# Attention, MoE and MLP in one kernel: query tiles of two chunks in reverse order, their causal mask added by GpSimd

## The chip, the cores and the metric

One NeuronCore of a Trainium2 chip runs the whole program. The metric is device time in microseconds, the median of several executions. The engines are TensorE (PE; its weight loads are listed as PEld), VectorE (DVE), ScalarE (ACT), GpSimd (POOL) and SyncE (SP, which here only issues DMAs).

## The reference, cut to what matters

```python
scores = (1/sqrt(D)) * q @ k^T                 # B, H, S, D = 2, 8, 576, 64
cum    = cumsum(log(clip(f, 1e-4, 1)), -1)
scores = scores + cum[:, :, :, None] - cum[:, :, None, :]
scores = where(j > i, -1e9, scores)            # causal mask
attn   = softmax(scores);  x = attn @ v        # x: 1152 tokens x 512
x      = sum_e p_e * relu(x @ w1[e]) @ w2[e]   # 4 experts, F = 1024
out    = gelu_sigmoid(x @ w_in) @ w_out        # d_ff = 2048
```

The term with the query's own `cum` is constant along a row, so softmax drops it: only the key side is added.

## The kernel before

Attention is cut into four chunks of queries: chunks 0 and 2 are rows 0 to 255 of batch 0 and 1, chunks 1 and 3 rows 256 to 575. Chunk 0 goes first, head by head, by a path of its own ("plain", `first_step`). The rest goes by pairs of heads: four pairs of chunk 1, then four pairs that hold chunks 2 and 3 of batch 1. A pair of chunk 1 or 3 has three units, one for each tile of 128 queries: q0 = 256 (384 keys), 384 (512 keys) and 512. The last holds 64 queries of each head side by side and all 576 keys, in two pieces of 288.

A unit passes through these steps, named here as in the rows: scores `s` (PE, line 652, products with a high and a low part of q, `qhi` and `qlo`); the maximum (DVE, line 682), which adds the gate rows to the scores, writes `e` and returns `mx`; exp (ACT, line 698); the norm (POOL, line 708, multiplies `e` by `sm`, the inverse sum); transposes `t` (PE, line 726); copies `ph` (ACT); the product with v, `x` (PE, line 756). The gate rows are `cum` broadcast over the partitions by DMA: `cb` (512 keys, one for each head, for the tiles below 512) and `cbs` (576 keys, two halves of 64 partitions, for the tile q0 = 512). `load_cum` loads them two units ahead of a pair; `cb` has four buffers, `cbs` two, so a pair's rows reuse those of the pair two before.

The mask before is a matmul: line 655 adds `identr` x `tri` (128x128, -1e10 above the diagonal) onto the diagonal block of the scores, `tri2` in the tile q0 = 512, and line 657 does both heads at once where there are at most 256 keys (chunk 2).

POOL also makes the pairs' operands: `ks` (line 578, low part of the keys, half on DVE), `qhi` (line 68) and `qlo` (line 596), three units ahead. Scores of a tile with over 256 keys take both of the two PSUM buffers `ps_s`.

Expert products fill PE between the units: first layer `m<-xh,whi` and its like (lines 951, 934), second layer line 1099. Their weights are split into `whi` (ACT, line 71) and `wlo` (DVE, line 249; four in chunk 0 on POOL). A scheduler sets the order on each engine when the program is built; an engine then runs its instructions strictly in that order.

Of the kernel before, what the change touches and what calls it, by code (L numbers as in the profile page):

```python
# [7 lines left out]
F32 = mybir.dt.float32  # L8
# [7 lines left out]
B, H, S, D = 2, 8, 576, 64  # L16
# [4 lines left out]
CH = [(0, 0, SA), (0, SA, SB), (1, 0, SA), (1, SA, SB)]  # L21
# [8 lines left out]
REST = EXP[2]  # L30
QW = {1: 768, 2: 512, 3: 768}
LEAD = 3
NTILE = NT // 128
NBLK = 12
NMOE = 8
# [15 lines left out]
def attn_moe_mlp(ctx: ExitStack, tc: tile.TileContext, qk0, qk1, qk2, v0, vp, fg, dp, wa_moe, wb_moe, wa_mlp, wb_mlp, out):  # L51
# [6 lines left out]
    nc = tc.nc  # L58
# [5 lines left out]
    def f(ap):  # L64
        return ap.bitcast(F32)
# [9 lines left out]
    def load(out, in_):  # L75

        ins = nc.sync.dma_start(out=out, in_=in_)
        if start[0]:
            tc.keep_in_program_order(ins)
# [44 lines left out]
    cb_p = pool("cb", 4, scope=att_scope)  # L124
    cbs_p = pool("cbs", 2, scope=att_scope)
# [3 lines left out]
    cumd = pool("cumd", 1, bass.MemoryType.DRAM).tile([16, S], F32, name="cumd")  # L129
# [12 lines left out]
    tri = ac.tile([128, 128], F32R, name="tri")  # L142
# [24 lines left out]
    seq = [(1,) + units[0], (2,) + units[0], (1,) + units[1]]  # L167
# [4 lines left out]
    for v_ in range(v_exp, len(visits)):  # L172
        b, cs = visits[v_]
# [327 lines left out]
    pass_of = {c: p for p in passes for c in p[0]}  # L501
    groups, heads, pairs = {}, {}, {}

    def plain(c):


        return c == 0
# [90 lines left out]
    def load_cum(p, h0):  # L598

        cs, b, s0 = p  # L600
        st = pairs[p, h0]
        r = b * H + h0
        st["cb"] = [cb_p.tile([128, 512], F32, tag="cb", name="cb") for _ in range(2)]
        for g, cb in enumerate(st["cb"]):
            load(cb, cumd[r + g:r + g + 1, :512].to_broadcast([128, 512]))
        st["cbs"] = cbs_p.tile([128, S], F32, tag="cbs", name="cbs")
        for g in range(2):
            load(st["cbs"][64 * g:64 * g + 64], cumd[r + g:r + g + 1, :].to_broadcast([64, S]))

    def units_of(c, h0):  # L610

        if plain(c):
            return [(c, ((h,), (0, 128))) for h in (h0, h0 + 1)]
        _, s0, n = CH[c]
        return [(c, ((h0, h0 + 1), (q0,))) for q0 in range(s0, s0 + n, 128)]

    sc, raw_s = {}, {}
    NEG = -1.0 / D ** 0.5
# [1 line left out]
    def emit_scores(c, u):  # L620


        hs, tiles = u
        out = []
        for q0 in tiles:
            w = min(q0 + 128, S)
            if plain(c):
                st = heads[c, hs[0]]
                mm = [(0, w, [(st["qd"][:, q0:q0 + 128], st["kd"][:, :w])])]
            else:  # L630
                p = pass_of[c]
                st = pairs[p, hs[0]]
                (hi, lo), o = st["qs", c], 2 * (q0 - CH[c][1])
                zs = [(0, w, (0,)), (0, w, (1,))] if q0 < 512 else [(0, 288, (0, 1)), (288, S, (0, 1))]
                mm = [(a, z, [(t[:, o + 128 * g:o + 128 * g + 128], st["ks"][:, g, a:z]) for g in gs for t in (hi, lo)])
                      for a, z, gs in zs]
            pts = []
            both = not plain(c) and w <= 256
            for a, z, _ in mm:
                if plain(c):  # L640
                    if q0 == 0:
                        bank = ps_s.tile([128, 512], F32, tag="s", name="s")
                    pts.append(bank[:, q0:q0 + w])
                else:
                    if not both or not pts:
                        bank = ps_s.tile([128, 512], F32, tag="s", name="s")
                    pts.append(bank[:, 256:256 + w] if both and pts else bank)
                out.append((q0, w, a, z, pts[-1]))
            n = len(mm[0][2])
            for i in range(n):  # L650
                for pt, (a, z, lr) in zip(pts, mm):
                    nc.tensor.matmul(pt[:, :z - a], lhsT=lr[i][0], rhs=lr[i][1], start=i == 0 and not (both and pt is not bank),  # L652
                                     stop=i == n - 1, skip_group_check=both)
                    if i == 0 and z == w and not plain(c) and not both:
                        nc.tensor.matmul(pt[:, q0 - a:w - a], lhsT=identr, rhs=tri2 if w == S else tri, start=False, stop=False)
                if both and i == 0:
                    nc.tensor.matmul(bank.rearrange("p (g k) -> p g k", g=2)[:, :, q0:w], lhsT=identr,
                                     rhs=tri.unsqueeze(1).to_broadcast([128, 2, 128]), start=False, stop=False,
                                     skip_group_check=True)
        raw_s[c, u] = out  # L660
# [193 lines left out]
    def attention():  # L854


        seq = unit_seq
        first, last = {}, {}
        for i, (c, u) in enumerate(seq):
            for h in u[0]:  # L860
                first.setdefault((pass_of[c], h - h % 2), i)
                last[c, h] = i
        first_q = {}
        for i, (c, u) in enumerate(seq):
            if True:
                first_q.setdefault((pass_of[c], u[0][0], c), i)
        nxt = list(first)
        per_unit = dict(scores=emit_scores, max=emit_max, exp=emit_exp, norm=emit_norm, tr=emit_tr)
        by_last = dict(pv=emit_pv, x2=emit_x2)
        names = sorted(STAGES, key=lambda k: -STAGES[k])  # L870
        for i in range(len(seq) + L_X2 + 1):
            done = None
            new = [k for k in nxt if first[k] == i + LEAD]
            new_q = [k for k, j in first_q.items() if j == i + LEAD]
            last_pool = [j for j in nc.cur_bb.bb.instructions if j.engine == nc.gpsimd.engine][-1]
            with tc.issue_after(last_pool) if i == 0 else ExitStack():
                for k in new:
                    prep_parts(*k)
                for k in new_q:
                    prep_queries(*k)  # L880
            for k in [k for k in nxt if first[k] == i + 2]:
                load_cum(*k)
            for k in [k for k in nxt if first[k] == i and i]:
                load_values(*k)
            for k in names:
                j = i - STAGES[k]
                if k in per_unit:
                    if 0 <= j < len(seq):
                        per_unit[k](*seq[j])
                    continue  # L890
                fn, at = by_last[k], last
                for key in list(at):
                    if at[key] == j:
                        fn(*key)
                        if k == "x2" and key[1] == H - 1:
                            done = key[0]
            for k in new:
                n = nxt.index(k) + 1
                if n < len(nxt):
                    load_heads(*nxt[n])  # L900
            yield done
# [615 lines left out]
```

## Time and profile before

| | |
|---|---|
| median of 3 runs (range) | 691.7 us (691.58 to 691.74) |
| profiled execution | 691.82 us |
| its span | 690.1 us |
| instructions | 11086 |
| PE busy | 681.2 us |
| POOL busy | 239.4 us |
| DVE busy | 531.4 us |

The span is what the profile of one execution covers; 1.7 us lie outside it. Matmuls are pipelined and their ends are modelled, so a busy PE isn't PE at its peak: progress is read from the starts of its instructions.

### The profile page before, as it was taken

How to read it: one execution, taken by the hardware profiler on the slowest of the kernel's cores; microseconds unless marked ns; L12 is line 12 of the kernel's file. 1: busy time of each engine (PE TensorE's matmuls, PEld its weight loads, DVE VectorE, ACT ScalarE, POOL GpSimd, SP SyncE). 2: the span in 40 equal slices, each digit the busy share in tenths (PEclk: the TensorE clock that was granted, in tenths of full speed). 3: DMA queues.
4: the chain of work that ended last, by engine and by line, in shares of the span. 5: the costliest groups of instructions: out<-in, count | busy, mean ns of one | idle time of the engine just before them, and what ended most of it. 6: DMA issues, size and time to landing. Idle time of an engine off the chain costs nothing.

```text
span 690.1 us, 11086 instructions
## 1 busy us (share of the span) xinstructions
PE 681.2 (99%) x3937; PEld 600.0 (87%) x3937; DVE 531.4 (77%) x1097; ACT 354.3 (51%) x821; POOL 239.4 (35%) x286
## 2 busy tenths in 40 slices
PE   8999999999999999999999999999999999999997
PEld 4797888888888998998889898898899998998986
DVE  6896777777789688676887878767799989998632
ACT  5778767667543645635246254362456454452420
POOL 6887576532233454543035324133003300120000
PEclk9999999999999999999999999999999999999999
DMA  8697726313542244144631422403332544441012
GB/s 251 229 301 249 258 93 238 99 61 93 168 138 61 51 134 129 48 128 157 196 107 47 144 86 82 146 33 107 123 107 77 153 138 136 154 153 61 1 47 91
DMA packets 41063, 87.59 MB, mean 127 GB/s; under 512 B 3720, under 2 KB 5776, under 8 KB 40752
## 3 DMA queue, kind: packets, MB, share of 16 engines
q1 hardware_dynamic: 40680, 84.75, 38.2%
q0 software_dynamic: 288, 2.10, 0.8%
q8 instruction: 31, 0.51, 0.3%
q14 instruction: 24, 0.20, 0.1%
q10 hardware_dynamic: 40, 0.04, 0.0%
HBM read 73.98 MB, written 12.88 MB: 126 GB/s over the span
## 4 chain that ended last, share of the span: by engine, by line
PE 92%; DVE 4%; POOL 1%; ACT 1%; DMA 1%; issue 1%; SPq 0%; POOLq 0%; DVEq 0%
PE m L1099 41%; PE m L974 23%; PE m L934 15%; PE s L652 4%; PE x L756 4%; PE t L726 3%; PE m L1255 1%; DMA dpraw<-in_dp_dram 1%; DVE acc L1143 0%; POOL ks L578 0%; DVE hl L1088 0%; DVE cvd L431 0%; DVE wlo L249 0%; PE m L951 0%; DVE wf L433 0%
## 5 line engine op out<-in xcount | busy, mean ns | idle before, releaser
L1099 PE MATMUL m<-whi,hh 128*128 128x512 f32 x392 | 109.6, 392 | 0.0
L1099 PE MATMUL m<-wlo,hh 128*128 128x512 f32 x392 | 108.0, 391 | 0.0
L1099 PE MATMUL m<-whi,hl 128*128 128x512 f32 x392 | 107.2, 390 | 0.0
L249 DVE TENSOR_TENSOR wlo<-wst,whi 128x512 fp32r<-128x512 f32 x132 | 100.3, 774 | 5.1 <-ACT whi L71 4.6
L985 POOL TENSOR_TENSOR hl<-jc,hh 128x320 fp32r<-128x320 f32 (+1 forms) x60 | 53.1, 888 | 141.1 <-ACT hh L71 141.1
L71 ACT ACTIVATE whi<-wst 128x512 fp32r<-128x512 f32 x136 | 80.7, 625 | 23.7 <-PE m L1099 13.5
L1099 PEld LDWEIGHTS m<-wlo,hh 128*128 128x128 f32 x392 | 73.4, 188 | 15.5
L1099 PEld LDWEIGHTS m<-whi,hl 128*128 128x128 f32 x392 | 73.5, 188 | 15.5
L1099 PEld LDWEIGHTS m<-whi,hh 128*128 128x128 f32 x392 | 71.9, 188 | 12.4
L270 POOL TENSOR_TENSOR sr<-wst 128x256 f32<-128x256 f32 x20 | 17.9, 893 | 156.2 <-DMA wst<-wm 58.0
L708 POOL TENSOR_SCALAR e<-e,sm 128x128 f32<-128x128 f32 (+4 forms) x72 | 46.7, 660 | 60.3 <-DVE sm L706 35.9
L983 ACT ACTIVATE jc<-jc 128x320 f32<-128x320 f32 (+1 forms) x60 | 27.1, 451 | 54.8 <-DVE jc L980 54.3
L1143 DVE SCALAR_TENSOR_TENSOR acc<-m,dpn,acc 128x512 f32<-128x512 f32 x63 | 46.5, 744 | 9.0 <-PE m L1099 8.9
L934 PE MATMUL m<-xh,whi 128*128 128x256 f32 (+2 forms) x256 | 51.7, 316 | 0.0
L934 PE MATMUL m<-xl,whi 128*128 128x256 f32 (+2 forms) x256 | 51.7, 316 | 0.0
L934 PE MATMUL m<-xh,wlo 128*128 128x256 f32 (+2 forms) x256 | 51.0, 313 | 0.0
L698 ACT ACTIVATE e<-e,mx 128x128 f32<-128x128 f32 (+4 forms) x72 | 41.7, 581 | 11.6 <-DVE mx L682 11.1
L934 PEld LDWEIGHTS m<-xh,whi 128*128 128x128 f32 x256 | 41.6, 189 | 1.4
L934 PEld LDWEIGHTS m<-xl,whi 128*128 128x128 f32 x256 | 41.5, 189 | 0.8
L1082 ACT ACTIVATE m<-m 128x384 f32<-128x384 f32 x48 | 23.0, 480 | 37.3 <-DVE m L980 35.6
L934 PEld LDWEIGHTS m<-xh,wlo 128*128 128x128 f32 x256 | 41.5, 189 | 0.7
L71 ACT ACTIVATE ph<-t 128x256 f32<-128x256 f32 (+4 forms) x81 | 28.9, 405 | 17.6 <-PE t L726 17.2
(173 smaller groups left out, 1502.5 us busy)
## 6 DMA issues: line engine op xcount, KB each, us to landing
wst<-in_wa_moe_dram SPq DMA_DIRECT2D x28, 512.0 KB, 3.8
wst<-in_wb_moe_dram SPq DMA_DIRECT2D x28, 512.0 KB, 4.5
mst<-in_wa_mlp_dram SPq DMA_DIRECT2D x16, 512.0 KB, 3.7
wm<-wf SPq DMA_DIRECT2D x32, 256.0 KB, 3.9
mst<-in_wb_mlp_dram SPq DMA_DIRECT2D x16, 512.0 KB, 4.1
wst<-wm SPq DMA_DIRECT2D x16, 512.0 KB, 3.9
cb<-cumd SPq DMA_DIRECT2D x16, 256.0 KB, 4.0
qr<-in_qk_dram SPq DMA_DIRECT2D x8, 384.0 KB, 5.1
```

Of the source, the lines that this page charges most:

```text
L71: return nc.scalar.activation(out=out, in_=in_, func=AF.Copy)
L249: (nc.gpsimd if v_ == 0 and kind == 'a' and g < 4 else nc.vector).tensor_sub(lf, raw, f(hf))
L652: nc.tensor.matmul(pt[:, :z - a], lhsT=lr[i][0], rhs=lr[i][1], start=i == 0 and not (both and pt is not bank), stop=i == n - 1, skip_group ...
L698: nc.scalar.activation(out=e[:, off:off + w], in_=e[:, off:off + w], func=AF.Exp, scale=-1.0, bias=mx, accum_out=sm[:, 0, k:k + 1])
L708: nc.gpsimd.tensor_scalar(out=e[:, off:off + w], in0=e[:, off:off + w], scalar1=sm[:, 0, i:i + 1], scalar2=1.0, op0=ALU.mult, op1=ALU.mult)
L756: nc.tensor.matmul(pt[64 * g:64 * g + 64, o:n], lhsT=lhsT, rhs=rhs, start=i == 0, stop=i == nk - 1)
L934: nc.tensor.matmul(p[:, :n], lhsT=w[:, k, :], rhs=x[c][:, k, :], start=(j == 0 and k == 0), stop=(j == 2 and k == 3))
L974: nc.tensor.matmul(p[:, :WN], lhsT=w[a][:, k, :], rhs=x[z][:, k, :], start=start and j == 0 and k == 0, stop=stop and j == 2 and k == 1, s ...
L983: nc.scalar.activation(out=r, in_=r, func=AF.Relu)
L985: nc.gpsimd.tensor_sub(hl[:, g, :], r, f(hh[:, g, :]))
L1099: nc.tensor.matmul(p, lhsT=h_tile(v_, b, c, j, x, k), rhs=wb[v_, k][w].rearrange("p a c -> p (a c)"), start=i == 0 and k == 0, stop=i == 2 ...
L1143: nc.vector.scalar_tensor_tensor(out=a, in0=p, scalar=d, in1=a, op0=ALU.mult, op1=ALU.add)
```

## The change

The tiles of chunks 1 and 3 (`MASKED`) run from last to first: 512, 384, 256. For the tiles 384 and 256 the mask matmul goes. Instead POOL adds `tri` in place to the diagonal block of both `cb` (`mask_next`), one tile ahead: when the unit q0 = 512 is begun, to columns 384 to 511; when the unit 384 is begun, to columns 256 to 383. A later (lower) tile doesn't read the columns that were masked for the one before it, since it has 128 keys fewer. The add for 256 has to wait until DVE's maximum of the tile 384 has read those columns without the mask, and the maximum of 256 waits for the add. The tile 512 keeps its matmul with `tri2`. In chunk 1 `cbs` is now loaded ahead of `cb`; in the pairs of batch 1, which begin with chunk 2, `cb` stays first.

```diff
--- before.py
+++ after.py
@@ -30,6 +30,7 @@
 REST = EXP[2]
 QW = {1: 768, 2: 512, 3: 768}
 LEAD = 3
+MASKED = (1, 3)
 NTILE = NT // 128
 NBLK = 12
 NMOE = 8
@@ -600,19 +601,32 @@
         cs, b, s0 = p
         st = pairs[p, h0]
         r = b * H + h0
-        st["cb"] = [cb_p.tile([128, 512], F32, tag="cb", name="cb") for _ in range(2)]
-        for g, cb in enumerate(st["cb"]):
-            load(cb, cumd[r + g:r + g + 1, :512].to_broadcast([128, 512]))
-        st["cbs"] = cbs_p.tile([128, S], F32, tag="cbs", name="cbs")
-        for g in range(2):
-            load(st["cbs"][64 * g:64 * g + 64], cumd[r + g:r + g + 1, :].to_broadcast([64, S]))
+        def load_long():
+            st["cb"] = [cb_p.tile([128, 512], F32, tag="cb", name="cb") for _ in range(2)]
+            for g, cb in enumerate(st["cb"]):
+                load(cb, cumd[r + g:r + g + 1, :512].to_broadcast([128, 512]))
+
+        def load_last():
+            st["cbs"] = cbs_p.tile([128, S], F32, tag="cbs", name="cbs")
+            for g in range(2):
+                load(st["cbs"][64 * g:64 * g + 64], cumd[r + g:r + g + 1, :].to_broadcast([64, S]))
+
+        for fn in (load_long, load_last) if cs[0] == 2 else (load_last, load_long):
+            fn()
 
     def units_of(c, h0):
 
         if plain(c):
             return [(c, ((h,), (0, 128))) for h in (h0, h0 + 1)]
         _, s0, n = CH[c]
-        return [(c, ((h0, h0 + 1), (q0,))) for q0 in range(s0, s0 + n, 128)]
+        return [(c, ((h0, h0 + 1), (q0,))) for q0 in range(s0, s0 + n, 128)[::-1 if c in MASKED else 1]]
+
+    def mask_next(c, u):
+
+        q0 = u[1][0] - 128
+        if c in MASKED and q0 >= CH[c][1]:
+            for cb in pairs[pass_of[c], u[0][0]]["cb"]:
+                nc.gpsimd.tensor_add(cb[:, q0:q0 + 128], cb[:, q0:q0 + 128], f(tri))
 
     sc, raw_s = {}, {}
     NEG = -1.0 / D ** 0.5
@@ -651,7 +665,7 @@
                 for pt, (a, z, lr) in zip(pts, mm):
                     nc.tensor.matmul(pt[:, :z - a], lhsT=lr[i][0], rhs=lr[i][1], start=i == 0 and not (both and pt is not bank),
                                      stop=i == n - 1, skip_group_check=both)
-                    if i == 0 and z == w and not plain(c) and not both:
+                    if i == 0 and z == w and not plain(c) and not both and (c not in MASKED or w == S):
                         nc.tensor.matmul(pt[:, q0 - a:w - a], lhsT=identr, rhs=tri2 if w == S else tri, start=False, stop=False)
                 if both and i == 0:
                     nc.tensor.matmul(bank.rearrange("p (g k) -> p g k", g=2)[:, :, q0:w], lhsT=identr,
@@ -894,6 +908,8 @@
                         fn(*key)
                         if k == "x2" and key[1] == H - 1:
                             done = key[0]
+            if i < len(seq):
+                mask_next(*seq[i])
             for k in new:
                 n = nxt.index(k) + 1
                 if n < len(nxt):
```

The counts of built instructions differ in two forms alone: 32 matmuls `s<-tri,identr` 128x128 are gone from PE, and 32 adds `cb<-cb,tri` 128x128 are new on POOL. The order changes on every engine. Three places:

POOL at the end of chunk 0, where it normalizes the last heads (`e<-e,sm`) and makes the last `wlo`. Before:

```order
L249 TENSOR_TENSOR wlo<-wst,whi 128x512
L708 TENSOR_SCALAR e<-e,sm 128x128
L708 TENSOR_SCALAR e<-e,sm 128x256
L249 TENSOR_TENSOR wlo<-wst,whi 128x512
L708 TENSOR_SCALAR e<-e,sm 128x128
```

Now:

```order
L250 TENSOR_TENSOR wlo<-wst,whi 128x512
L629 TENSOR_TENSOR cb<-cb,tri 128x128
L722 TENSOR_SCALAR e<-e,sm 128x128
L722 TENSOR_SCALAR e<-e,sm 128x256
L250 TENSOR_TENSOR wlo<-wst,whi 128x512
L629 TENSOR_TENSOR cb<-cb,tri 128x128
L690 MEMSET e 128x64
L722 TENSOR_SCALAR e<-e,sm 128x128
```

Two adds (pair 1's first ones, each behind the landing of its `cb`) and a memset now stand ahead of norms of chunk 0.

POOL in the pairs of chunk 1, from pair 2's `qlo` (the second `qlo` buffer) on. Before:

```order
L596 TENSOR_TENSOR qlo_1_133<-qr,qhi 64x3x128 x2
L708 TENSOR_SCALAR e<-e,sm 128x384 x2
L708 TENSOR_SCALAR e<-e,sm 128x512 x2
L68 TENSOR_SCALAR qhi<-qr 128x768
L578 TENSOR_TENSOR ks<-kq,ks 64x576
L596 TENSOR_TENSOR qlo_0_132<-qr,qhi 64x3x128 x2
L708 TENSOR_SCALAR e<-e,sm 128x576
```

Now:

```order
L597 TENSOR_TENSOR qlo_1_133<-qr,qhi 64x3x128 x2
L629 TENSOR_TENSOR cb<-cb,tri 128x128 x3
L722 TENSOR_SCALAR e<-e,sm 128x576
L629 TENSOR_TENSOR cb<-cb,tri 128x128
L690 MEMSET e 128x64
L69 TENSOR_SCALAR qhi<-qr 128x768
L629 TENSOR_TENSOR cb<-cb,tri 128x128
L597 TENSOR_TENSOR qlo_0_132<-qr,qhi 64x3x128 x2
L579 TENSOR_TENSOR ks<-kq,ks 64x576
L722 TENSOR_SCALAR e<-e,sm 128x512 x2
```

Of the first three adds two are pair 2's for its tile 384; the third and the fourth are pair 1's for its tile 256. The add behind `qhi` is pair 3's: it waits for a `cb` of pair 3, and pair 3's `qlo` and `ks` and pair 1's norms (128x512, its tile 384) are behind it.

PE at pair 1's second and third unit. Before:

```order
L652 MATMUL s<-ks,qhi 128x512
L655 MATMUL s<-tri,identr 128x128
L652 MATMUL s<-ks,qlo_0_132 128x512
L1099 MATMUL m<-whi,hh 128x512 x2
L652 MATMUL s<-ks,qhi 128x288
```

Now:

```order
L666 MATMUL s<-ks,qhi 128x512
L666 MATMUL s<-ks,qlo_0_132 128x512
L666 MATMUL s<-ks,qhi 128x384
L666 MATMUL s<-ks,qlo_0_132 128x384
L1115 MATMUL m<-whi,hl 128x512 x4
L950 MATMUL m<-xh,whi 128x256 x4
L950 MATMUL m<-xh,wlo 128x256 x4
L950 MATMUL m<-xl,whi 128x256 x4
L740 MATMUL t<-identr,e 128x128 x5
```

The mask's 128-column matmul no longer stands between the high and the low product, and the five transposes of the tile 512 are now the first of the pair.

## Rows read from the trace of the kernel before

**Rows 1.** The page, part 1: busy time of each engine, share of the span, instructions.

```profile
PE 681.2 (99%) x3937; PEld 600.0 (87%) x3937; DVE 531.4 (77%) x1097; ACT 354.3 (51%) x821; POOL 239.4 (35%) x286
```

**Rows 2.** Waits of PE over the span: us in total, times, longest.

```profile
PE t L726 <- POOL e L708: 1.4, 1, 1.4
PE s L652 <- POOL qlo L596: 0.3, 1, 0.3
```

**Rows 3.** Windows: us, then PE, PEld, DVE, ACT, POOL busy, clock, DMA.

```profile
40.00:60.00 20.00, 20.00 (x156) 18.35 (x155) 17.87 (x51) 15.19 (x38) 18.41 (x21) 1.00 0.72 243
140.00:160.00 20.00, 20.00 (x143) 16.66 (x142) 14.82 (x47) 14.80 (x42) 6.09 (x10) 1.00 0.09 29
```

**Rows 4.** Groups of PE by form: line, operation, tiles, shape, count, busy us, mean ns.

```profile
L655 PE MATMUL s<-tri,identr 128*128 128x128 f32 x32 | 7.4, 232 | 0.0
```

**Rows 5.** Chain that ended last, in order of time: start us, us, what.

```profile
91.54 0.83 PE m L934 x7
...
235.41 10.90 PE m L1099 x48
```

**Rows 6.** Timeline of PE at pair 1: start us, us, instruction.

```profile
30.34 0.44 PE L652 MATMUL s<-ks,qhi 128*128 128x384 f32 x1
...
34.52 0.40 PE L652 MATMUL s<-ks,qhi 128*128 128x512 f32 x1
...
34.81 0.45 PE L652 MATMUL s<-ks,qlo 128*128 128x512 f32 x1
35.10 0.64 PE L1099 MATMUL m<-whi,hh 128*128 128x512 f32 x2
```

**Rows 7.** Groups of POOL by form, as in Rows 4.

```profile
L985 POOL TENSOR_TENSOR hl<-jc,hh 128x256 fp32r<-128x256 f32 x18 | 14.4, 807 | 42.2 <-ACT hh L71 42.2
...
L708 POOL TENSOR_SCALAR e<-e,sm 128x128 f32<-128x128 f32 x16 | 5.8, 371 | 6.7 <-DVE sm L706 5.1 <-PE x L756 1.4
```

**Rows 8.** Timeline of POOL at the end of chunk 0.

```profile
19.75 1.27 POOL L249 TENSOR_TENSOR wlo<-wst,whi 128x512 fp32r<-128x512 f32 x1
...
26.35 0.83 POOL L708 TENSOR_SCALAR e<-e,sm 128x128 f32<-128x128 f32 x2 [1.43 <-PE x L756]
27.26 1.74 POOL L578 TENSOR_TENSOR ks<-kq,ks 64x576 fp32r<-64x576 f32 x1
```

**Rows 9.** Tile cbs, 13 to 15 us: issues, and time to landing.

```profile
L77 SPq DMA_DIRECT2D cbs<-cumd x2: 468/475/482, 13.5 to 14.1; - x2
...
DMA to landing us min/median/max: 7.9/7.9/7.9
```

**Rows 10.** Timeline of POOL in chunk 1.

```profile
36.08 2.75 POOL L596 TENSOR_TENSOR qlo<-qr,qhi 64x384 fp32r<-64x384 f32 x2
40.67 3.36 POOL L708 TENSOR_SCALAR e<-e,sm 128x384 f32<-128x384 f32 x4 [1.84 <-DVE sm L706]
44.01 1.32 POOL L68 TENSOR_SCALAR qhi<-qr 128x768 fp32r<-128x768 f32 x1
45.42 1.74 POOL L578 TENSOR_TENSOR ks<-kq,ks 64x576 fp32r<-64x576 f32 x1
47.21 2.43 POOL L596 TENSOR_TENSOR qlo<-qr,qhi 64x384 fp32r<-64x384 f32 x2
```

**Rows 11.** Tile cbs, 34.55 to 36 us (pair 2): issues, time to landing.

```profile
L77 SPq DMA_DIRECT2D cbs<-cumd x2: 450/522/594, 34.6 to 35.1; - x2
...
DMA to landing us min/median/max: 5.1/5.2/5.2
```

**Rows 12.** Tile cb, 39 to 42.8 us (pair 3): time to landing.

```profile
DMA to landing us min/median/max: 6.7/6.7/6.7
```

**Rows 13.** The page, part 6: DMA issues, KB each, median us to landing.

```profile
cb<-cumd SPq DMA_DIRECT2D x16, 256.0 KB, 4.0
```

**Rows 14.** Timeline of DVE, two subtractions of line 249.

```profile
27.63 1.92 DVE L249 TENSOR_TENSOR wlo<-wst,whi 128x512 fp32r<-128x512 f32 x1
...
39.15 0.68 DVE L249 TENSOR_TENSOR wlo<-wst,whi 128x512 fp32r<-128x512 f32 x1
```

## The prediction

> **What bounds the kernel now.** I read the page's busy times first: PE works 99% of the span, POOL 35% [rows 1]. Since a busy PE is a modelled one, the list of PE's waits comes next: 1.4 us for POOL's norms and 0.3 us for POOL's `qlo` are the largest in the attention with pairs [rows 2]. So PE sets the time nearly everywhere, and each matmul taken off it shortens the span, as long as no other engine makes it wait. The windows say where one could: from 40 to 60 us POOL is busy 18.41 us of 20 and DVE 17.87; from 140 to 160 us POOL only 6.09 [rows 3]. The change takes work from PE everywhere in the pairs and gives it to POOL, which has no room in the first pairs and plenty in the later ones.
>
> **What goes from PE.** 32 mask matmuls, 128 columns each. The group says 232 ns each, 7.4 us together [rows 4], but that is time from start to modelled end. What one costs is seen between starts. A unit's 512-key head starts at 34.52 and the expert product behind it at 35.10: 0.58 us for high product, mask and low product [rows 6]. In a steady run a 512-column matmul takes 10.90 / 48 = 0.227 us [rows 5], two take 0.454, so the mask costs 0.13 us. By its columns alone, a quarter of 512, it would be 0.06; the rest falls on the matmuls beside it. 32 x 0.13 = **4.2 us gained**; bounds 32 x 0.06 = 1.9 and the group's 7.4. I take the middle one, since it covers the whole sequence that becomes shorter.
>
> **What POOL gets.** 32 adds of 128x128, a form with two inputs that the trace doesn't have. Below it lies one input at the same size, 371 ns, above it two inputs at twice the columns, 807 ns [rows 7]. I take 0.5 us, 16 us in all. About 13 adds fall before 70 us, 19 behind; the latter I cost at nothing, because POOL is mostly idle there [rows 3]; uncovered they would be 9.5 us of POOL, of which PE would see what its filler can't hide.
>
> **End of chunk 0.** The first add stands behind the `wlo` that ends at 19.75 + 1.27 = 21.0 us [rows 8] and needs pair 1's `cb`, which is now issued where `cbs` was, at 13.5 and 14.1, and lands 7.9 us later, at 21.4 and 22.0 [rows 9]. So POOL waits 0.4, then two adds and a memset cost 1.2. Behind them stand norms of chunk 0, and behind these the transposes. But POOL idles 1.43 us ahead of the last norm, at 26.35, and `ks` of pair 1 follows at 27.26 [rows 8]; of 1.6 us all but 0.2 is covered there. PE in between has other products and catches up later in part. I take **0.3 us lost**; bounds 0 (PE's filler covers it) and 1.6.
>
> **Pair 1's first transposes.** Pair 2's `qlo` ends at 36.08 + 2.75 = 38.8 [rows 10]. The two adds behind it need pair 2's `cb`, now issued at 34.6 and 35.1 in the place of `cbs`: landing 39.7 and 40.3 at 5.1 and 5.2 us [rows 11]. With the third add POOL is free at 41.3 and the norm of the tile 512 (about 0.84, a quarter of the 3.36 us for four norms [rows 10]) ends at 42.1. PE now reaches these transposes after 24 matmuls of 512 columns for experts and 4 for scores (28 x 0.227 = 6.4), 24 of 256 (0.83 / 7 = 0.119 each [rows 5], 2.9), eight of 288 and two of 384 between these two prices (about 1.4): 10.7 us from 30.34 [rows 6], plus the 0.3 us `qlo` wait that stays and 0.3 from chunk 0: 41.6. **0.5 us lost.** Before, POOL idled 1.84 us here [rows 10], which the adds use up.
>
> **Pair 1's second transposes.** This is the largest cost. POOL does a fourth add and `qhi` until 44.0 and then stands before pair 3's add. Pair 3's `cb` reuses pair 1's; pair 1's is now read last by the maximum of the tile 256, which itself waits for the third add (41.3) and ends near 42. The load lands a median of 4.0 us later [rows 13], at 46.0; in the trace this pair's took 6.7 [rows 12], which would make 48.7. Then add 0.5, `qlo` 2.43, `ks` 1.74 [rows 10], norm 0.84: 51.5. PE arrives, from 42.1, after the five transposes (0.6, at the 0.119 of a 256-column product), 36 matmuls of 256 (4.3), four of 512 (0.9) and ten of 288 or 384 (1.4): 49.3. **2.2 us lost**; without the wait POOL would be done at 49.5 and the loss 0.2, with the longer landing it is 4.9. What waits behind the add is also queued on SP: the second `cb` of pair 3 needs the second maximum, and expert weights stand behind it in SP's queue, so ACT's `whi` comes late with it, at about the same time as the norm.
>
> **Later.** Pair 2's tile 256 is normalized behind pair 4's `qhi`, `ks`, `qlo` and two adds; I take **0.6 us** more, a little over one add. From there POOL catches up.
>
> **What goes with it.** The wait of 1.4 us for the norms [rows 2] lies in this stretch before and has its place in another order now: I count it as gone.
>
> The sum: -4.2 + 0.3 + 0.5 + 2.2 + 0.6 - 1.4 = **-2.0 us**. The profiled execution took 691.82, so 689.8; the median shown is 0.1 below it: **689.7 us**.
>
> **A page against the row.** DVE's `wlo` takes 0.68 us at 39.15 and 1.92 at 27.63, while POOL makes `ks` (27.26 to 29.00) [rows 8, 14]. That is held time, not slower work. The Trainium skill, "SBUF — State Buffer", section "Who interferes with whom", says that a DVE instruction with two SBUF inputs contends with a GpSimd instruction that reads SBUF, and that the one that comes second is blocked for the other's whole length. By that rule each add can hold a `wlo`; the trace's pair above agrees. In rows alone: 13 adds of 0.5 us before 70 us hold DVE by up to 6.5 us, where it has 2.1 us free in 20 [rows 3]. If half of that reached PE, some 2 us, the sum would be 0.
>
> **Rivals.** First, *POOL becomes the bound* and the change costs time: add the long landing (4.9 for 2.2, +2.7) and adds of 0.8 us instead of 0.5 (13 x 0.3 = 3.9, of which PE sees most while POOL is full). -2.0 + 2.7 + 3.0 gives 695.5; it decides from the point where POOL's backlog at pair 1's second transposes passes the 4.2 us that PE saves. For it speaks the full POOL at 40 to 60 us, against it the later idle time. Chance 0.22. Second, *the gain is small*: the masks cost 0.06 us each, 1.9 us in all, and the waits come as above: +0.3, 692.1. For it: the mask streams only a quarter of the columns of its neighbours; against it the 0.58 us of the whole sequence. Chance 0.15. Third, *the adds hold DVE*, as worked out above, and some 2 us of it reach PE: 691.7. For it the held `wlo`, against it that DVE works ahead of PE on most weights. Chance 0.10. Fourth, *the waits don't arise*, because pair 3's `cb` lands with little other traffic and the first transposes are covered: -4.2 + 0.8 - 1.4, 687.0, or a little better with a dearer mask. Chance 0.15. My forecast, 688 to 690.3, has 0.38.
>
> **Chances.** 0.2%, 1.4 us, is about what a measurement of this kernel tells from no change. Faster takes my forecast and the fourth case, 0.53; same takes the second and the third, 0.25; slower the first, 0.22. The range for 8 in 10 leaves out the dearest tenth of the first case and the best of the fourth: 686.5 to 693.5; the likeliest case's own range is 688 to 690.3.
>
> **What the trace would show.** No matmul of 128 columns at the score lines except in chunk 2; pitch of high to low product 0.23 us; POOL busy 16 us more, each add near 0.5. The adds of pair 3 should stand behind an idle POOL of some 2 us near 44 to 46 us, with a wait for `cb`; PE's waits for norms should sum to 3 to 4 us, all before 75 us, and none behind that. I am wrong if PE waits long at POOL or DVE behind 80 us (then the late adds weren't covered), if DVE's maximum of a tile 256 often waits for its add, or if the last product with v comes so late that chunk 3's first layer waits, which now has 15 instead of 24 second-layer matmuls between.

## The result, and the profile after

The changed kernel is slower: 698.25 us (median of 4 runs, 698.1 to 699.97) against 691.72 (691.58 to 692.64) in the same set, ratio 1.0094, 95% interval 1.008 to 1.0109. Its profiled execution took 698.28 us. 689.7 us was forecast, and 698.25 lies outside the range. Two executions of experiments below, at a mean granted clock of 0.66 and 0.56, took 954 and 1120 us and are left out of the medians.

The page and the waits of PE, as in [rows 1, 2]:

```profile
span 696.5 us, 11056 instructions
PE 685.7 (98%) x3904; PEld 599.2 (86%) x3905; DVE 531.0 (76%) x1097; ACT 355.9 (51%) x821; POOL 250.8 (36%) x318
```

```profile
PE t L740 <- POOL e L722: 2.3, 1, 2.3
...
PE t L814 <- POOL e L722: 1.1, 3, 0.4
PE s L666 <- DVE mx L696: 0.6, 2, 0.4
```

From 15 us on PE's listed waits grew from 2.1 us ([rows 2] and 0.4 for norms of chunk 0) to about 4, while the span grew by 6.4. So more than half of the loss is no wait: PE works longer (busy 685.7 us after 681.2, with 32 matmuls fewer). Where, is seen from the starts of the matmuls in both traces. The table gives by how much a kernel lags behind the kernel before when it has done the same matmuls (each shape at one price, masks not counted); the columns are the times in the kernel before. So the table is an estimate, good to about half a microsecond; the changed kernel's entry at 50 us is the softest, 1.2 to 2.3 by the prices taken. The experiments' kernels come below.

| us behind the kernel before, at | 28 | 37 | 50 | 54 | 86 | 124 | 185 | 249 us |
|---|---|---|---|---|---|---|---|---|
| changed kernel | 1.5 | 1.3 | 1.2 | 5.0 | 4.5 | 5.8 | 5.3 | 6.2 |
| order_alone | -0.2 | 1.2 | 1.0 | 2.0 | 3.1 | 4.1 | 6.2 | 7.1 |
| sums_late | -0.2 | 1.4 | 1.3 | 3.4 | 2.9 | 3.8 | 2.7 | 3.6 |
| heads_1_0 | 0.3 | 1.6 | 1.4 | 2.8 | 6.1 | 7.0 | 3.2 | 5.8 |
| order_and_heads | -0.2 | 1.1 | 1.2 | 2.3 | 4.4 | 4.3 | 1.6 | 3.8 |
| before_heads_2 | -0.1 | -0.2 | -0.2 | -0.4 | -0.4 | -1.2 | -3.2 | -3.2 |
| no_masks | -0.6 | -0.6 | -0.8 | -0.6 | -1.8 | -2.3 | -4.1 | -4.1 |
| chunk3_only | -0.1 | -0.1 | -0.2 | -0.4 | 0.0 | -1.3 | -5.1 | -2.5 |
| order_heads_rows_later | -0.2 | 1.1 | 1.5 | 1.4 | 0.8 | 4.6 | 1.9 | 4.1 |

The changed kernel loses 1.3 us up to 37 us and 2.7 to 3.8 between 50 and 54. From there to 185 us it wins nothing, though 24 of the 32 masks (pairs 3 and 4, and chunk 3) fall there. Two places, then.

**Pair 1's second transposes.** POOL, then PE, in the order of time; then the windows (us, then PE, PEld, DVE, ACT, POOL busy, clock, DMA):

```profile
48.54 0.57 POOL L629 TENSOR_TENSOR cb<-cb,tri 128x128 f32<-128x128 f32 x1 [3.03 <-DMA cb<-cumd]
49.08 2.11 POOL L597 TENSOR_TENSOR qlo<-qr,qhi 64x384 fp32r<-64x384 f32 x2
51.26 1.40 POOL L579 TENSOR_TENSOR ks<-kq,ks 64x576 fp32r<-64x576 f32 x1
52.76 1.37 POOL L722 TENSOR_SCALAR e<-e,sm 128x512 f32<-128x512 f32 x2
```

```profile
50.78 0.40 PE L666 MATMUL s<-ks,qlo 128*128 128x512 f32 x1
53.51 1.33 PE L740 MATMUL t<-identr,e 128*128 128x128 f32 x8 [2.33 <-POOL e L722]
```

```profile
52.00:54.00 2.00, 0.49 (x4) 0.42 (x4) 0.00 (x0) 0.66 (x2) 1.90 (x3) 1.00 1.05 410
54.00:56.00 2.00, 1.87 (x12) 1.42 (x11) 1.72 (x4) 1.47 (x3) 2.00 (x4) 0.73 0.96 315
56.00:58.00 2.00, 2.00 (x11) 2.00 (x10) 1.56 (x4) 1.42 (x4) 2.00 (x4) 0.50 0.24 74
58.00:60.00 2.00, 2.00 (x13) 1.36 (x11) 0.36 (x1) 1.29 (x4) 1.93 (x4) 0.92 0.00 0
```

This is the forecast chain: the add for pair 3 waits for its gate rows, `qlo`, `ks` and the norm stand behind it, PE waits 2.33 us. Not foreseen is what follows: behind a stretch with 0.49 us of work in 2, the granted clock goes down to 0.50 (1.2 GHz) for some 2 us. Before, it is 1.00 here [rows 3]. By the clock column that is 0.54 + 1.0 + 0.16 = 1.7 us of TensorE's time. How much longer the run gets by it is not shown: of the four executions the one with a mean granted clock of 1.000 took 698.22 us, the profiled one, at 0.998, 698.28.

**The products with v.** The chain that ended last, before and then after, at one pair each (start us, us, what):

```profile
83.44 2.21 PE x L756 x20
85.64 0.81 PE t L726 x6
```

```profile
89.82 0.68 PE x L770 x2
90.50 0.59 PE t L740 x4
...
92.74 1.39 PE m L1115 x6
94.13 2.20 PE x L770 x16
96.33 0.69 PE t L740 x5
```

Each product leaves two records. Before, a pair's ten products are one block of 2.21 us. They go in turn to the two heads, each on one half of TensorE's columns (64 of 128), and the trace has the two starts of a couple 0.007 us apart, the next couple 0.27 us later: two at a time. After, the first product (head 0, first 128 keys) goes ahead alone, then transposes, and the other nine are out of step: 0.68 + 2.20 = 2.88 us (the block has 18 records; the chain passes through 16 of them). The cause is the order of units. The pair's last unit was the tile 512, whose `ph` of both heads is copied from one tile of transposes; now it is the tile 256 with two heads one after the other, and head 0's first product is ready while head 1 still has copies to come; heads_1_0 below tests this. Summed over all products (each from its start to the next matmul's start, at most 0.45 us), they take 26.5 us before and 31.1 after.

### The profile page after: what moved, and what is told of

The parts are those of the page before. It is cut to its first block, busy times and chain, and to the rows that moved or that the text cites. A ratio compares the mean times of both kernels' runs of the same rounds, so it can differ in the third digit from the quotient of the medians.

```text
span 696.5 us, 11056 instructions
## 1 busy us (share of the span) xinstructions
PE 685.7 (98%) x3904; PEld 599.2 (86%) x3905; DVE 531.0 (76%) x1097; ACT 355.9 (51%) x821; POOL 250.8 (36%) x318
## 4 chain that ended last, share of the span: by engine, by line
PE 89%; DVE 4%; DMA 2%; POOL 2%; ACT 1%; issue 1%; SPq 0%; POOLq 0%; ACTq 0%; DVEq 0%
PE m L1115 40%; PE m L990 22%; PE m L950 15%; PE x L770 4%; PE s L666 3%; PE t L740 3%; DMA kq<-in_qk_dram 1%; POOL e L722 1%; DMA wst<-in_wa_moe_dram 1%; PE m L1271 1%; DMA dpraw<-in_dp_dram 1%; PE m L967 1%; DVE hl L1104 1%; DVE acc L1159 0%; DVE wlo L250 0%
## 5 line engine op out<-in xcount | busy, mean ns | idle before, releaser
L72 ACT ACTIVATE whi<-wst 128x512 fp32r<-128x512 f32 x136 | 80.6, 623 | 22.5 <-PE m L1115 13.3
L722 POOL TENSOR_SCALAR e<-e,sm 128x128 f32<-128x128 f32 (+4 forms) x72 | 43.6, 619 | 42.2 <-DVE sm L720 18.1
L1028 ACT ACTIVATE u<-m 128x320 f32<-128x320 f32 (+2 forms) x26 | 11.2, 432 | 50.5 <-PE m L990 50.5
```

Source lines behind the costliest of these rows:

```text
L72: return nc.scalar.activation(out=out, in_=in_, func=AF.Copy)
L722: nc.gpsimd.tensor_scalar(out=e[:, off:off + w], in0=e[:, off:off + w], scalar1=sm[:, 0, i:i + 1], scalar2=1.0, op0=ALU.mult, op1=ALU.mult)
```

## The experiments

Each ran in five rounds beside the kernel before, whose median was 691.5 to 692.3 in these sets. "Products" is the sum just named.

### One: the order, the heads, the sums

heads_1_0 (changed kernel, in `emit_pv`):

```diff
-            for g in range(2):
+            for g in ((1, 0) if c in MASKED else (0, 1)):
```

> The changed kernel with one edit: in chunks 1 and 3 the product with v takes head 1 of the pair before head 0 at each step over the keys, so that its first matmul is one of the head whose probabilities come last and cannot start alone. Theory A (the new order of tiles makes the first product of head 0 run alone, and then the two heads' products, which ran side by side before, get out of step: 2.88 us in place of 2.21 for a pair, eight pairs): 698.2 - 5.4 = 692.9 us, and every group of products with v is one unbroken block of about 2.2 us. Rival B (the loss is the masks' sums on GpSimd and their waits, and the products only look longer): within 1 us of the changed kernel, 697 to 699.

697.66 us (1.0072, 1.0059 to 1.0086). The products are blocks again (25.4 us), as theory A says, and the time hardly moves, as B says. Both can be read from the table: from 124 to 185 us this kernel gains 3.8 us, where the changed one gains 0.5. But at 86 us it has a new stall. Timelines of ACT and PE, then a window:

```profile
89.11 1.15 ACT L72 ACTIVATE whi<-wst 128x512 fp32r<-128x512 f32 x2 [2.81 <-DMA wst<-in_wb_moe_dram]
90.16 0.71 ACT L712 ACTIVATE e<-e,mx 128x512 f32<-128x512 f32 x1
```

```profile
91.74 1.22 PE L950 MATMUL m<-xh,whi 128*128 128x256 f32 x4 [3.02 <-DVE hl L1104]
94.80 2.27 PE L770 MATMUL x<-ph,vd 128*64 128x320 f32 x20
```

```profile
92.00:94.00 2.00, 2.00 (x10) 2.00 (x11) 1.47 (x9) 1.98 (x6) 1.06 (x2) 0.50 0.32 73
```

ACT stands 2.81 us at weights that land late, with exp and `hh` queued behind; PE runs dry for 3 us and then at half clock.

order_alone (the reversed tiles and loads, all masks on PE, no adds):

```diff
-                    if ... and not both and (c not in MASKED or w == S):
+                    if ... and not both:
-            if i < len(seq):
-                mask_next(*seq[i])
```

> The changed kernel without the sums on GpSimd: all 32 masks are matmuls on TensorE as before, but the tiles still go from last to first and the last tile's gate rows are still loaded first. Theory A (products out of step in 7 of the 8 pairs, here too): 691.7 + 7 x 0.67 = 696.4 us, without a wait of pair 1's second transposes above 1.5 us. Rival B (the sums on GpSimd are the whole loss): 691 to 692.5 us.

699.07 us (1.0096, 1.0082 to 1.0109), no faster than the changed kernel. The loss doesn't need the adds on POOL: the order of tiles and loads costs 7 us by itself, and what the adds cost is about what the masks give. Products 31.0 us. Rival B is out. The rest begins at 34 us, at pair 1's second scores:

```profile
35.46 0.50 PE L666 MATMUL s<-ks,qhi 128*128 128x512 f32 x1 [0.96 <-DVE mx L696]
```

The tile 512 now comes first and holds both score buffers until DVE, which is in the middle of weights, has made its maximum. In the table, every kernel with the tile 512 first has this lag of 1.1 to 1.6 us by 37 us, those without POOL's delay in chunk 0 too. (The changed kernel comes to this place 1.5 us late already, and waits only 0.17 us there.)

heads_in_turn (kernel before, chunks 1 and 3: all keys of head 0, then all of head 1):

```diff
-        for i in range(nk):
...
-            for g in range(2):
+        for i, g in ([(i, g) for i in range(nk) for g in range(2)] if c not in (1, 3) else
+                     [(i, g) for g in range(2) for i in range(nk)]):
```

> The kernel before with one edit: in chunks 1 and 3 the product with v does all of head 0 and then all of head 1, in place of the two heads in turn. Measures by itself what side by side is worth. Theory A (two products of different heads run at the same time on the two halves of TensorE's columns, the first of a couple starting 0.007 us before the second): a pair's block goes from 2.2 to about 4.2 us, eight pairs, 691.7 + 16 = 708 us. Rival B (the engine takes them one after another whatever their order, and only the records of their starts lie close): 691 to 693 us.

704.33 us (1.0175, 1.016 to 1.0191), products 40.3. Side by side is real. In the timeline a block now runs from 85.97 until the next transposes at 89.84:

```profile
85.97 3.94 PE L756 MATMUL x<-ph,vd 128*64 128x320 f32 x20
89.84 0.88 PE L726 MATMUL t<-identr,e 128*128 128x128 f32 x6
```

That is 3.87 us for the 2.21 of before, 1.66 more for each of eight pairs, 13.3. The time grew by 12.3 and not by the 16 expected: in the trace head 1's first product starts at 87.643 us, beside head 0's products of 192 and 64 columns, so the two heads still overlap there. The Trainium skill, "TensorEngine Tiling (Array Packing)", section "Tiling Modes", says that the array can be divided into two tiles of 128x64 whose matmuls run in parallel. The trace agrees: 2.21 us in turn, 3.87 one head after the other.

sums_late (changed kernel, in `mask_next`; `norms` holds the norms' instructions):

```diff
+                if len(norms) > 1:
+                    tc.add_manual_dep(getattr(ins, "ins", ins), norms[-2].name, ... NoSync ...)
```

> The changed kernel with one edit: each unit's sums on GpSimd may only be issued behind the division of the probabilities of the unit two before it, so that the sum for pair 3 that waits 3.03 us for its gate rows at 48.5 us no longer stands ahead of pair 2's query and key rounding and of the division that pair 1's second transposes wait for. Theory A (this stall costs 2.3 us of wait and 1.7 us at the lower clock after it): 698.2 - 3 to 4 = 694 to 695.5 us, with the granted clock at 1.00 from 50 to 60 us; the products with v stay out of step. Rival C (the wait for the gate rows only moves to another place in the queue, or another engine is late there anyway): 697 to 699 us.

695.93 us (1.0058, 1.0044 to 1.0071), 2.3 us gained: theory A's way, but less than the 3 to 4 it expected. PE's waits from 40 to 70 us:

```profile
PE m L957 <- ACT whi L72: 1.7, 1, 1.7
PE t L747 <- POOL e L728: 0.2, 1, 0.2
```

The wait for POOL is gone, and a wait for rounded weights is there instead; it is shorter, and the clock stays at 1.00 from 50 to 60 us. So this stall has two legs, as rival C holds: without the adds' leg the kernel is 2.3 us faster, and the weights' leg is left.

### Two: mends together, and a control

heads_and_late is sums_late with head 1 first in chunks 1, 2 and 3; order_and_heads is order_alone with head 1 first in 1 and 3. before_heads_2 is the kernel before with one edit:

```diff
-            for g in range(2):
+            for g in ((1, 0) if c == 2 else (0, 1)):
```

> The changed kernel with both mends: GpSimd's sums only behind the division two units before (as in sums_late), and the product with v takes head 1 first in chunks 1, 2 and 3. Theory A (the products out of step cost 4.6 to 5.7 us in all, whatever else goes on): 695.9 - 5 = 691 us, unless a new wait of TensorE of several us shows as in heads_1_0 (there 3.02 us behind weights that landed late). Rival D (the products are out of step because the two heads' copies come at different times, so that waiting for both only turns the same loss into a wait): 695 to 697 us with waits of x for ph in the eight pairs.

> order_alone (all masks on TensorE, tiles from last to first, last tile's gate rows first) with head 1 first in the product with v in chunks 1 and 3. Theory A (what the order costs is the products with v): 699.1 - 5 = 694 us; what is left over the kernel before is the first tiles' wait for the maximum at 34 us, about 1 us, and 1 us of others. Rival E (the order costs by waits of transposes and loads): 698 to 700 us.

> The kernel before with one edit: in chunk 2, whose tiles each hold two separate heads there too, head 1 first in the product with v. In the kernel before the first product of chunk 2's head 0 stands alone in the four pairs. Theory A: a lone 128x256 product costs about 0.25 to 0.3 us, four pairs: 691.9 - 1.1 = 690.8 us (690.3 to 691.3). Rival D: within 0.3 us of the kernel before.

before_heads_2: 688.70 us (0.9955, 0.9943 to 0.9967). It is faster than both kernels, by 3.2 us instead of the 1.1 expected. The kernel before already had the same fault in chunk 2. Its chain, and that of before_heads_2, at the first of the four pairs:

```profile
108.85 0.58 PE x L756 x2
109.42 0.48 PE t L726 x3
...
110.38 0.80 PE x L756 x5
```

```profile
109.56 0.80 PE x L756 x8
```

0.58 us a pair, 2.3 for four, are in these rows (products 26.5 to 24.3); no wait takes the remaining 0.9, so it should lie in the matmuls around them; that isn't shown. Until 86 us nothing moves in the table, and no new wait appears. This is the cleanest evidence for theory A, at three times the size it expected.

order_and_heads: 696.43 (1.0061, 1.0049 to 1.0073), between A and E: products 25.1, 2.6 us gained of 5.9. heads_and_late: 692.57 (1.0008, 0.9995 to 1.0021), same as before. Beside sums_late that is 3.4 us, no more than chunk 2 gave before_heads_2. So in the turned kernels the products' time comes back, and more than half of it is lost again. Part of that is waits for late weights, 3.0 us in order_and_heads (1.4 in order_alone), and the clock: behind its wait of 2.03 us, which ends at 66.62 us, it lacks 0.30 + 1.0 + 0.40 = 1.7 us by these windows (columns as above):

```profile
66.00:68.00 2.00, 1.38 (x9) 1.38 (x10) 1.40 (x4) 2.00 (x4) 0.29 (x1) 0.85 1.01 395
68.00:70.00 2.00, 2.00 (x8) 1.71 (x7) 1.50 (x6) 2.00 (x7) 0.45 (x1) 0.50 0.99 355
70.00:72.00 2.00, 2.00 (x11) 1.67 (x11) 0.32 (x2) 1.23 (x3) 1.12 (x3) 0.80 0.29 110
```

Why the weights are late, ACT shows, and SyncE ahead of it:

```profile
65.94 1.15 ACT L72 ACTIVATE whi<-wst 128x512 fp32r<-128x512 f32 x2 [3.59 <-DMA wst<-in_wa_moe_dram]
```

```profile
42.82 4.62 SPq L78 DMA_DIRECT2D cb<-cumd  x2
47.53 0.39 SPq L78 DMA_DIRECT2D wst<-in_wa_moe_dram  x1
...
58.97 1.14 SPq L78 DMA_DIRECT2D cb<-cumd  x2
60.20 1.06 SPq L78 DMA_DIRECT2D wst<-in_wa_moe_dram  x1
```

The gate rows of pairs 3 and 4 wait for buffers at the head of SyncE's queue, with weights behind them. The kernel before issues these rows at 39.3 and 52.3 us: there a pair's `cb` is last read by its second unit, here by its third. The weights behind them move from 42.8 and 57.9 us to 47.5 and 60.2.

shared_tile_last (tiles 384, 256, 512; adds one unit earlier; both mends):

```diff
+        return [t[1], t[0], t[2]] if c in MASKED else t
```

> The masks stay on GpSimd, but the tiles go 384, 256, 512: the sum for tile 384's own keys is made before it, that for 256's after it, and the last tile, which has gate rows of its own, is the last unit of a pair as in the kernel before; the gate rows of the first two tiles are loaded first; sums behind the division two units before, head 1 first in the product with v. Theory A (the loss is in where the shared tile stands, the masks are worth 2 to 3 us): the products with v take 25.5 us in all, no wait above 1.5 us in pair 1: 689 to 690 us, below the kernel before. Rival C (a sum that stands right ahead of the tile that needs it holds up DVE, since gate rows land only 1 to 2 us before): 692 to 696 us with waits of s or t for mx or cb in each pair.

694.86 us (1.0035, 1.0022 to 1.0048): in time rival C. Products 24.6, but 3.3 us lag by 37 us. The waits are not the ones that rival C named, for maxima and gate rows, but those for weights and `qlo`:

```profile
PE m L963 <- ACT whi L72: 3.4, 2, 2.3
PE s L677 <- POOL qlo L597: 1.6, 2, 1.1
```

### Three: what the masks are worth

no_masks (kernel before; the condition of line 654 gets `and w == S`), and the change for fewer pairs: later_pairs (pairs 3 and 4 of chunk 1, and chunk 3), chunk3_only, chunk3_sums_late (as the last, with the dependency of sums_late); these three with head 1 first in chunks 1 to 3:

```diff
+        return c in MASKED and (c == 3 or h0 >= 4)      # later_pairs
+        return c == 3                                   # chunk3_only, chunk3_sums_late
```

> The kernel before without the 32 mask matmuls that the change takes from TensorE, and nothing in their place: the first tiles' scores stay unmasked, so part of the computation is left out, and what is timed is the whole gross gain that the masks can give. Theory F (a mask matmul takes 0.06 us of TensorE, the step from its start to the next start, and what follows it is not lengthened by it): 691.9 - 2.0 = 689.9 us. Theory G (the prediction's term, 0.13 us for each): 691.9 - 4.2 = 687.7 us.

> The change for the later pairs alone: pairs 1 and 2 of chunk 1 keep the order, loads and mask matmuls of the kernel before; pairs 3 and 4 of chunk 1 and the four of chunk 3 go from last to first with the sums on GpSimd, behind the division two units before; head 1 first in the product with v in chunks 1 to 3. Theory A (the waits of the change all belong to pair 1 and 2, and the order costs nothing where the products stay side by side): progress like the kernel before up to 64 us, 24 masks at 0.06 us below before_heads_2: 688.7 - 1.5 = 687.2 us. Rival C (a new wait for weights or sums in the later pairs, as at 220 us in heads_and_late): 689 to 692 us. No gain over before_heads_2 would say that masks on GpSimd are worth nothing here even where nothing waits for them.

> The change in chunk 3 alone (its four pairs go from last to first, their 16 masks are sums on GpSimd); chunk 1 keeps order, loads and masks of the kernel before; head 1 first in the product with v in chunks 1 to 3. To be set beside before_heads_2 (688.7 us). Theory A (with the products side by side, a mask taken from TensorE is worth 0.115 us, as no_masks gave for 32, wherever no new wait arises; GpSimd is busy 1.8 of 2 us only up to 80 us): 688.7 - 1.8 = 686.9 us. Rival C (turned order and sums bring waits of their own in these pairs too): 689 to 692 us.

> chunk3_only with the sums issued only behind the division two units before. Theory A: as chunk3_only, 686.5 to 687.5 us, since in chunk 3 the gate rows are there long before. Rival C, if its waits come from sums that stand ahead of rounding and divisions on GpSimd: below chunk3_only by 1 us or more.

no_masks: 688.01 (0.995, 0.9938 to 0.9963). 3.7 us, 0.11 for each of 32: theory G, the prediction's way of reading the cost, not the 0.06 from start to start. (Its trace is 4.1 us ahead, 0.6 of it before the first mask.) later_pairs: 692.28 (1.001, 0.9998 to 1.0023), rival C; in its profiled execution, the longest of twelve at 695.52, PE waits 2.0 us for a norm in chunk 1 again. chunk3_only: 689.32 (0.9965, 0.9952 to 0.9979); chunk3_sums_late: 689.01 (0.9961, 0.9949 to 0.9974). Both beat the kernel before, not before_heads_2. The table says where: at 185 us chunk3_only is 1.9 us ahead of before_heads_2, as much as 16 masks at 0.115 are, and then loses 2.6, most of it at 225 to 235 us, in expert products some 30 us behind the end of attention. Two of the pieces, in chunk3_sums_late:

```profile
224.49 0.56 PE L1000 MATMUL m<-xh,sh 128*128 128x320 f32 x2 [0.47 <-DVE jc L1006]
...
228.00 0.56 PE L1000 MATMUL m<-th,sl 128*128 128x320 f32 x2 [0.32 <-DVE sl L304]
```

The sums being late or not makes no difference there (0.3 us).

### Four: who holds the weights

Two levers on SyncE's queue. "Rows later" issues `cb` of pairs 3 and 4 one unit later, which puts one weight piece ahead of it; "6 rows" gives `cb` six buffers and `cbs` one (the edits in part):

```diff
+            for k in [k for k in nxt if i and first[k] == i + 1 and k[0][0][0] != 2]:
+                load_cum(*k, 1)
```

```diff
-    cb_p = pool("cb", 4, scope=att_scope)
-    cbs_p = pool("cbs", 2, scope=att_scope)
+    cb_p = pool("cb", 6, scope=att_scope)
+    cbs_p = pool("cbs", 1, scope=att_scope)
```

> order_and_heads (all masks on TensorE, tiles from last to first, products with v side by side; 696.4 us) with one edit: the gate rows of the first two tiles of pairs 3 and 4 are issued one unit later, which puts one weight piece ahead of them on SyncE's queue, and nothing else. Theory H (turned round, the gate rows of a pair are last read by its last unit, so the next pair's rows wait for the buffer at the head of SyncE's queue, until 60 us for pair 4 where the kernel before issues them at 52 us; the weights behind them land late, ScalarE waits 3.59 us for them at 65.9 us and TensorE 2.5 us): the two waits for the rounded weights at 52.8 and 64.2 us go, 696.4 - 3 = 693.4 us. Rival I (the weights' piece waits for its own buffer, the rows ahead of it are not what holds it): 696 to 697 us.

> The changed kernel with the same edit alone (one weight piece ahead of the gate rows of pairs 3 and 4 on SyncE's queue). In the changed kernel TensorE does not wait for weights in these pairs, but GpSimd waits for the rows; a later issue of them can only lengthen that. Theory H: no gain or a loss, 698 to 700 us, with the wait for GpSimd's sum at 48.5 us as long or longer. Rival J (whatever empties SyncE's queue sooner gains): 695 to 697 us.

> heads_and_late (692.6 us) with the same edit. There TensorE waits 2.0 us for the rounded weights at 52.7 us and 1.0 us at 65.8 us. Theory H: both go, 692.6 - 2.5 = 690 us, which is below the kernel before. Rival I: 692 to 693 us. Rival C (the later rows now hold up the sums and the divisions behind them): 693 to 695 us.

> order_and_heads (696.4 us) with six buffers in place of four for the gate rows of the first two tiles, and one in place of two for those of the last tile (the place for it), and no other edit; SyncE's queue has the same order. Theory H (pair 3's and pair 4's gate rows wait at the head of SyncE's queue for a buffer that the turned order frees one unit later, and the weights behind land late): pair 3's rows are issued right behind the last tile's, at about 41 us in place of 42.8 to 47.4, and pair 4's near 52 in place of 59 us; TensorE's waits for the rounded weights at 52.8 and 64.2 us go: 693 us. Rival I (the weights wait for buffers of their own, or the queue is held elsewhere): 696 to 697 us.

> The changed kernel with the same edit of the buffers alone (six and one). Theory H: GpSimd's sum for pair 3 no longer waits 3.03 us for its rows at 48.5 us, TensorE's wait of 2.33 us at 53.5 us and the lower clock behind it go: 698.2 - 3.5 = 694.7 us; the products with v stay out of step. Rival C (another wait takes their place): 697 to 698.5 us.

> heads_and_late (692.6 us) with the same edit of the buffers (six and one): all mends together. Theory H: the waits for the rounded weights of 2.0 and 1.0 us at 52.7 and 65.8 us go: 690 us; with masks at 0.115 us each, and 3.2 us of chunk 2's products with v (before_heads_2), the change would reach 691.9 - 3.7 - 3.2 = 685 us if no wait were left. Rival I: 692 to 693 us.

Rows later: 696.60 (1.0069, 1.0053 to 1.0084), 698.08 (1.0081, 1.0067 to 1.0094) and 697.42 (1.0073, 1.0058 to 1.0088). Theory H missed the time in the first, which lies in rival I's range, and in the third, which lies above all three. The stall does move: order_heads_rows_later lags 0.8 us at 86 us, where order_and_heads lags 4.4, but it is back at 4.6 by 124 us. In the changed kernel the time is what H said and the reason wrong: the wait for the norm fell to 1.0 us.

6 rows: 696.97 (1.0078, 1.0065 to 1.0091), 702.75 (1.016, 1.0147 to 1.0173) and 698.01 (1.0096, 1.007 to 1.0122). H missed all three, and the probe was a poor one: with one buffer, `cbs` takes `cb`'s place at the head of the queue. In after_6_rows, SyncE and ACT:

```profile
38.25 1.09 SPq L78 DMA_DIRECT2D cbs<-cumd  x2
39.39 1.05 SPq L78 DMA_DIRECT2D cb<-cumd  x2
40.54 0.38 SPq L78 DMA_DIRECT2D wst<-in_wb_moe_dram  x1
```

```profile
47.47 0.63 ACT L72 ACTIVATE whi<-wst 128x512 fp32r<-128x512 f32 x1 [4.48 <-DMA wst<-in_wb_moe_dram]
```

In the changed kernel pair 2's `cbs` is issued at 33.2 us. Here it is 5 us later, and the weights behind it too.

## Why the prediction was wrong, by its own steps

- **What goes from PE**: -4.2 forecast, -3.7 measured (no_masks). Nearly right; its cheaper bound was not.
- **What POOL gets**: 0.5 us an add; the group has 0.6, 19.0 us in all. Of the 20 adds behind 70 us (19 forecast) none makes PE wait: its list has no wait from 75 to 250 us.
- **End of chunk 0** and **first transposes**: 0.8 together, 1.3 measured at 37 us, ahead of these transposes, which then waited for nothing. The adds do delay chunk 0 (1.5 us at 28 us), but without them the same lag comes from another place: order_alone and sums_late have none at 28 us and wait 1.0 us for the first tile's maximum at 35. The prediction has no term for that wait.
- **Second transposes**: 2.2 forecast, a wait of 2.33 at the named place by the named chain. That the two agree is in part luck: the add began at 48.5 us, where the sum took 46.0 (48.7 was its dearer case), and PE came at 51.2 us instead of 49.3. And the term was mis-sized, 2.7 to 3.8 us by the table, since it had no clock in it.
- **Later** 0.6 and the **old wait** -1.4: no wait of either kind is in the trace after.
- **The step that failed** is the list of parts itself. The prediction followed what the new order does on POOL and SP and took PE's other work as unchanged. It has no term for the products with v, +4.6 us by the starts of the matmuls, nor for the first tile's wait. The forms were counted and their number was the same; their order was not looked at.

Terms as measured: -3.7 + 1.3 + 3.8 + 4.6 = 6.0, where the table has 6.2 and the medians 6.5. This fits better than it should: the two terms in the middle, read from the lag, already hold the gain of the masks before 54 us and pair 1's products.

Of the signs of being wrong that the prediction named none came: PE waits 3.4 us for norms, all before 75 us, and DVE waits 0.4 us for an add, once. They watched the adds, and none of them the products.

Rival one, POOL as the bound, had the right sign and part of the cause, the chain at pair 1's second transposes; but without adds on POOL the time is 699.07. Rival three, adds that hold DVE: DVE's busy time is unchanged (531.0 after 531.4), and PE waits 0.6 us for maxima (0.9 before); no such cost is seen. What the trace has is the reverse. The 11 adds that began while DVE was in a `wlo` took 0.67 to 0.93 us; of the other 21, 19 took 0.46 or 0.47. So here it is the add that is held. One such pair:

```profile
54.00 0.69 DVE L250 TENSOR_TENSOR wlo<-wst,whi 128x512 fp32r<-128x512 f32 x1 [2.25 <-ACT whi L72]
54.09 0.93 POOL L629 TENSOR_TENSOR cb<-cb,tri 128x128 f32<-128x128 f32 x1
```

That mending the products gives back 4.6 us was my own theory after the result, and it held only stage by stage (124 to 185 us), in heads_in_turn and in before_heads_2. In the turned kernels as a whole 0.6 to 2.6 us came back. What stays open is the other half of the turned order's price: order_and_heads, without adds and with its products in step, is still 4.4 us slower. Its lag is 1.1 us at 37 us, the first tile, and 3.3 more at 86 us, where it has the waits for late weights and the lower clock behind them; these waits move with the gate rows' issue but were not taken away by any kernel here. By 185 us it gets 2.8 back, and behind that it loses 2.2, of which 1.4 by 190 us; neither is explained by its list of waits. And no run parts the order of the tiles from that of the loads.

## What to carry to other kernels

When units are put in another order, look at every consumer of two of them, not only at the edited step: matmuls that share TensorE by halves of its columns lose time as soon as one can start before its partner (here 2.88 us for 2.21, and 3.87 where nearly all run alone). Issuing the later-ready one first keeps the couple together. In the kernel before that brought 3.2 us without a new wait, more than the change aimed at; in heads_1_0 the products were together and the time hardly moved. An in-order load queue makes a buffer's last reader part of the path of whatever is queued behind it. And a stall of TensorE is to be priced with the lower clock that may follow it.

## What the runs showed of the hardware

One record of a product with 64 columns (320 moving) takes 0.27 us alone (from start to start, in heads_in_turn), and two side by side take the same (in the kernel before). And the lower clock did not follow every stall: at the same place sums_late went on at 1.00 behind its wait of 1.7 us for weights, and heads_and_late, which has the same wait at 1.8 us, fell to 0.50. A window of sums_late, then three of heads_and_late:

```profile
54.00:56.00 2.00, 1.29 (x11) 1.29 (x12) 1.31 (x4) 1.98 (x4) 0.45 (x1) 1.00 1.05 414
```

```profile
52.00:54.00 2.00, 0.97 (x6) 0.59 (x5) 0.66 (x3) 0.98 (x3) 2.00 (x5) 1.00 1.03 397
54.00:56.00 2.00, 1.27 (x6) 1.27 (x7) 1.29 (x4) 1.95 (x4) 0.38 (x1) 0.68 1.04 409
56.00:58.00 2.00, 2.00 (x11) 2.00 (x10) 1.83 (x6) 1.54 (x5) 1.90 (x4) 0.50 0.43 126
```

The runs of heads_and_late lie from 691.4 to 696.2 us, wider than those of the kernel before. The eight with a mean granted clock of 0.999 or 1.000 took 691.4 to 692.8, the four with 0.995 to 0.997 took 693.1 to 696.2; the clock goes with the spread, but that it makes the spread was not shown.
